# Two exps trade places on ScalarE in the second half of the last head

## The chip, the cores and the metric

The kernel runs on one core of a Trainium2 chip. The metric is the device time of one execution in microseconds, of which the profiled span is 1.7 to 2.8 us less. Executions of one kernel scatter by 3 to 4 us here, so the median of a few runs is given for time.

## The reference, cut to what matters

One token goes through layer norm, attention over a cache of 32768 keys and values in each of 32 heads of 192, an output projection with residual, and a small MLP with residual.

```
q = (layernorm(x) @ wq).reshape(32 heads, 192)
scores = einsum("hd,hkd->hk", q, k_cache) * 192**-0.5
p = softmax(scores)
o = einsum("hk,hkd->hd", p, v_cache)
h = x + o.reshape(1, 6144) @ wo
out = h + relu(layernorm(h) @ w1) @ w2
```

Keys and values are 825 MB, and each is used once. Reading them is the bulk of the time: the DMA row of the page is at 90% or more in every slice but the last, at 429 GB/s over the span.

Of the kernel before, what the change touches and what calls it, by code (L numbers as in the profile page):

```python
# [80 lines left out]
def kernel(  # L81
# [48 lines left out]
    def chunks(h):  # L130
        return ends if h == LAST else full
# [469 lines left out]
    def copies(g, h, c):  # L601
        ld, off, jc, jp = chunks(h)[c][:4]
        t0 = sum(len(tiles(q[3])) for q in chunks(h)[:c])
        for k, (b0, nb) in enumerate(tiles(jp)):
            g.wait("T", h, c, k)
            src = tp[(t0 + k) % TP]
            g.do(lambda: act.copy(out=kT[c % 2][:, b0:b0 + nb, :], in_=src[:, 0:nb, :].bitcast(bf16)),  # L607
                 "act_pe", ("cp", h, c, k))

    def exp_pe(g, h, c):  # L610
        jp = chunks(h)[c][3]
        g.wait("S", h, c)
        g.do(lambda: act.activation(out=pB[c % NB][:, 0:jp], in_=sp[:, 0:jp], func=F.Exp, scale=SCALE,  # L613
                                    accum_out=dsums[:, 2 * c + 1:2 * c + 2]), "act_pe", ("ep", h, c))

    def exp_dve(g, h, c):
        ld, off, jc, jp = chunks(h)[c][:4]
        jd = jc - jp
        if jd == 0:
            return  # L620
        g.wait("sc", h, c)
        g.do(lambda: act.activation(out=pA[c % NB][:, 0:jd], in_=sc[c % NC][:, 0:jd], func=F.Exp, scale=SCALE,  # L622
                                    accum_out=dsums[:, 2 * c:2 * c + 1]), "act_pe", ("ed", h, c))

    def q_wide(g, h):
        g.wait("qs", h)
        if h > 0:
            g.wait("sc", h - 1, NC - 1)
        g.do(lambda: act.copy(out=qb[:], in_=mm[:, 0:Dh]), "act_dve", ("qb", h))
        g.do(lambda: act.copy(out=qm[:], in_=mm[:, Dh:Dh + 12]), "act_pe", ("qm", h))  # L630
# [13 lines left out]
    def act_head(g, h):  # L644
        q_wide(g, h)

        n = len(chunks(h))
        for c in range(n):
            if c == 4 and h < LAST:
                exp_pe(g, h, 3)  # L650
                exp_dve(g, h, 3)
                copies(g, h, 4)
                continue
            copies(g, h, c)
            if h == LAST:
                if c > 5:
                    exp_dve(g, h, c - 2)
                if c > 2:
                    exp_pe(g, h, c - 1)
                if c < 2:  # L660
                    exp_pe(g, h, c)
                    exp_dve(g, h, c)
                elif 2 < c < 5:
                    exp_dve(g, h, c - 1)
            elif c > 0:
                exp_pe(g, h, c - 1)
                exp_dve(g, h, c - 1)
        if h == LAST:
            exp_dve(g, h, n - 2)
        exp_pe(g, h, n - 1)  # L670
        exp_dve(g, h, n - 1)

    def act_end(g):
        act_head(g, LAST)
        act_norm(g, "ln2")
        g.wait("h1")
        g.wait("rs", "ln2")
        g.do(lambda: act.activation(out=h1T[:], in_=o_ps[:, 0:FT], func=F.Relu, scale=ln_t["ln2"]["rs"][:]),
             "act_pe", ("h1T",))
# [118 lines left out]
    for f in (dma_program, pool_program):  # L798
        f(plan)
    parts = {"pe": (pe_start, pe_head, pe_end), "act": (act_start, act_head, act_end), "dve": (dve_start, dve_head, dve_end)}  # L800
    logs, links = {}, {}
    for e, (start, head, end) in parts.items():
# [13 lines left out]
    for e in parts:  # L816
        far = {s: 0 for s in TAKEN[e]}
        ends_at[e] = []
        for h in range(LAST):
            for label in logs[e][h]:  # L820
                s, n = at[label]
# [86 lines left out]
```

## The kernel before: what the change and the argument touch

Each head is worked in chunks of keys. In a chunk some rows' scores are made on VectorE (multiply by the query into `pr`, reduce into `sc`); the others on TensorE: transposes into PSUM (`tp`), copies of them to SBUF by ScalarE (`kT`), then matmuls with two columns into the PSUM bank `sp`. ScalarE takes the exp of both: `exp_pe` of TensorE's scores (`sp` to `pB`), `exp_dve` of VectorE's (`sc` to `pA`). TensorE then multiplies both with the values into `o_ps`.

The last head has ten chunks, numbered 0 to 9; "the second half" is chunks 6 to 9. Its ScalarE program:

```
def act_head(g, h):
    q_wide(g, h)
    n = len(chunks(h))
    for c in range(n):
        ...                                # cut: chunk 4 of the other heads
        copies(g, h, c)                    # kT <- tp, waits for transposes of chunk c
        if h == LAST:
            if c > 5:
                exp_dve(g, h, c - 2)       # waits for VectorE's scores of chunk c-2
            if c > 2:
                exp_pe(g, h, c - 1)        # waits for TensorE's scores of chunk c-1
            ...                            # cut: chunks 0 to 4
    if h == LAST:
        exp_dve(g, h, n - 2)
    exp_pe(g, h, n - 1)
    exp_dve(g, h, n - 1)
```

There is one `sp` bank, so TensorE's scores of a chunk wait for the exp of the chunk before:

```
def scores_pe(g, h, c):
    g.wait("cp", h, c, ...)                # its copies
    if c > 0:
        g.wait("ep", h, c - 1)             # exp_pe of the chunk before has read sp
    ...
```

TensorE's order at the end:

```
        scores_pe(g, h, 6)
        transposes(g, h, 8)
        scores_pe(g, h, 7)                 # waits for exp_pe(6)
        transposes(g, h, 9)
        values(g, h, 4)
        scores_pe(g, h, 8)
        scores_pe(g, h, 9)                 # waits for exp_pe(8) and copies(9)
        for c in (5, 6, 7):
            values(g, h, c)
        den_mm(g, h)                       # sums of all exps
        values(g, h, 8)
        values(g, h, 9)
        ...                                # cut: scaling, projection, norm, MLP
```

The softmax here doesn't subtract the row's maximum and nothing guards it: scores larger than these inputs give would overflow.

## Time and profile before

| | before |
|---|---|
| median of 3 runs | 1922.56 us (1920.89 to 1924.06) |
| profiled span | 1920.8 us |
| last load that the chain names ends | 1850.08 us |
| VectorE's last scores end | 1902.59 us |
| last value product ends | 1909.87 us |
| from there to the end | 10.9 us |

The page's first part gives each engine's busy time. No engine is near full, and this says nothing about the end of the program: the average covers the 1850 us up to the last load that the chain names, in which the DMA row is full.

```profile
PE 1558.5 (81%) x15890; PEld 1090.5 (57%) x15890; DVE 1563.3 (81%) x732; ACT 938.0 (49%) x1998; POOL 1.0 (0%) x6
```

The DMA row, the chain of waits in order of time, the timeline of the last 30 us and the clock windows are shown and read in the prediction. PE is TensorE's matmuls, PEld its weight loads, DVE VectorE, ACT ScalarE, POOL GpSimd; a q behind such a name is that engine's sequencer. In the timeline a line is: start, duration, engine, source line, operation, output and input, count, and in brackets how long the engine idled before it and what ended that.

### The profile page before, as it was taken

What the parts mean: (1) busy time and instruction counts of PE and PEld (TensorE: products, weight loads), DVE (VectorE), ACT (ScalarE), POOL (GpSimd) and SP (SyncE); (2) the same over time, 40 slices, a digit from 0 to 9 for tenths busy, and PEclk for the clock granted to TensorE, in tenths of its full rate; (3) what the DMA queues carried; (4) which work ended last, traced back from release to release, by engine and by line L of the source; (5) the groups of instructions that cost most, each with busy time, mean ns of one, the idle gap of its engine ahead of it and who ended that gap; (6) DMA issues with size and microseconds to landing.
All of it is one profiled execution on the core that took longest, in us unless ns stands there. A gap on an engine that the chain in (4) does not pass through costs nothing.

```text
span 1920.8 us, 36095 instructions
## 1 busy us (share of the span) xinstructions
PE 1558.5 (81%) x15890; PEld 1090.5 (57%) x15890; DVE 1563.3 (81%) x732; ACT 938.0 (49%) x1998; POOL 1.0 (0%) x6
## 2 busy tenths in 40 slices
PE   7778787887888788888878878878788788888787
PEld 7555555555555565655555556555555556555554
DVE  2797787987878978789887889878798787897896
ACT  2455454554544554545545545535455455455453
POOL 0000000000000000000000000000000000000000
PEclk9888998888988889888899887899888898888898
DMA  9999999999999999999999999999999999999997
GB/s 410 425 437 427 430 438 430 440 427 436 432 434 432 439 429 431 436 431 441 427 440 427 437 429 436 438 426 437 431 437 427 441 428 439 428 436 437 427 433 320
DMA packets 29634, 825.29 MB, mean 430 GB/s; under 512 B 3115, under 2 KB 4652, under 8 KB 8108
## 3 DMA queue, kind: packets, MB, share of 16 engines
q1 hardware_dynamic: 29610, 824.98, 99.6%
q8 instruction: 15, 0.25, 0.0%
q14 instruction: 7, 0.06, 0.0%
q10 hardware_dynamic: 2, 0.00, 0.0%
HBM read 824.97 MB, written 0.00 MB: 429 GB/s over the span
## 4 chain that ended last, share of the span: by engine, by line
DVE 42%; DMA 37%; PE 14%; ACT 5%; issue 1%; DVEq 0%; POOLq 0%; SPq 0%
DMA kt<-in_A_k_cache_dram 35%; DVE sc L704 20%; DVE pr L701 20%; PE o_ps L364 7%; PE tp L383 6%; ACT kT L607 4%; DMA va<-in_A_v_cache_dram 2%; DVE o_pair L716 1%; PE sp L364 1%; ACT pA L622 0%; DVE oT L726 0%; DMA kt<-in_A_wq_dram 0%; DVE rec L709 0%; DVE rec L710 0%; DVE odd L722 0%
## 5 line engine op out<-in xcount | busy, mean ns | idle before, releaser
L701 DVE TENSOR_TENSOR pr<-kt,qb 128x3072 f32<-128x3072 bf16 (+2 forms) x257 | 757.5, 2948 | 314.9 <-POOLq L325 286.8
L607 ACT COPY kT<-tp 128x1024 bf16<-128x1024 bf16 (+1 forms) x897 | 812.9, 1016 | 276.8 <-PE tp L383 276.8
L383 PE MATMUL tp<-ident_f,kt 128*128 128x128 f32 x3453 | 590.9, 332 | 237.6 <-POOLq L346 163.2
L704 DVE TENSOR_REDUCE sc<-pr 128x16 f32<-128x3072 f32 (+2 forms) x257 | 756.9, 2945 | 8.9
L383 PEld LDWEIGHTS tp<-ident_f,kt 128*128 128x128 f32 x3453 | 486.0, 171 | 288.1 <-POOLq L346 168.9
L364 PE MATMUL o_ps<-va,pB 128*2 128x384 bf16 x1150 | 223.8, 343 | 62.8 <-POOLq L346 62.8
L364 PEld LDWEIGHTS sp<-qm,kT 128*128 128x128 bf16 x6906 | 197.6, 98 | 84.6 <-issue 42.8
L364 PE MATMUL sp<-qm,kT 128*128 128x2 bf16 x6906 | 214.4, 164 | 27.5 <-ACT pB L613 26.1
L364 PE MATMUL o_ps<-vb,pB 128*2 128x384 bf16 x1152 | 214.5, 332 | 22.2 <-ACT pA L622 21.6
L622 ACT ACTIVATE pA<-sc 128x16 bf16<-128x16 f32 (+2 forms) x257 | 58.0, 226 | 349.7 <-DVEq L65 349.7
L613 ACT ACTIVATE pB<-sp 128x16 bf16<-128x16 f32 (+2 forms) x258 | 51.8, 201 | 306.0 <-PE sp L364 306.0
L364 PEld LDWEIGHTS o_ps<-va,pB 128*2 128x2 bf16 x1150 | 94.5, 87 | 159.6 <-POOLq L346 70.3
L364 PE MATMUL o_ps<-va,pA 128*2 128x384 bf16 x898 | 174.9, 337 | 0.0
L364 PE MATMUL o_ps<-vb,pA 128*2 128x384 bf16 x896 | 166.7, 326 | 0.0
L364 PEld LDWEIGHTS o_ps<-vb,pB 128*2 128x2 bf16 x1152 | 90.2, 85 | 122.6 <-ACT pA L622 27.7
L364 PEld LDWEIGHTS o_ps<-va,pA 128*2 128x2 bf16 x898 | 78.4, 87 | 78.7 <-issue 13.6
L364 PEld LDWEIGHTS o_ps<-vb,pA 128*2 128x2 bf16 x896 | 75.3, 84 | 70.3
L613 ACT ACTIVATION_READ_ACCUMULATOR pB<-sp 128x1 f32 x258 | 54.8, 212 | 0.0
L622 ACT ACTIVATION_READ_ACCUMULATOR pA<-sc 128x1 f32 x257 | 52.8, 205 | 0.0
L364 PE MATMUL o_ps<-xn_ln,kt 128*96 128x1 bf16 (+1 forms) x316 | 22.3, 208 | 2.7 <-DMA kt<-in_A_wq_dram 2.7
L364 PEld LDWEIGHTS o_ps<-xn_ln,kt 128*96 128x96 bf16 (+1 forms) x316 | 22.1, 174 | 2.8 <-issue 2.7
L716 DVE TENSOR_SCALAR o_pair<-o_ps,rec 2x384 bf16<-2x384 f32 x32 | 19.4, 605 | 2.7 <-PE o_ps L364 1.7
(69 smaller groups left out, 186.8 us busy)
## 6 DMA issues: line engine op xcount, KB each, us to landing
kt<-in_A_k_cache_dram SPq DMA_DIRECT2D x62, 6144.0 KB, 26.7
vb<-in_A_v_cache_dram SPq DMA_DIRECT2D x63, 3072.0 KB, 20.8
va<-in_A_v_cache_dram SPq DMA_DIRECT2D x31, 6144.0 KB, 26.8
kt<-in_A_k_cache_dram SPq DMA_DIRECT2D x3, 3072.0 KB, 21.0
wo_s<-in_A_wo_dram SPq DMA_DIRECT2D x16, 480.0 KB, 19.0
kt<-in_A_wq_dram SPq DMA_DIRECT2D x4, 1536.0 KB, 10.9
va<-in_A_v_cache_dram SPq DMA_DIRECT2D x1, 3072.0 KB, 23.1
va<-in_A_v_cache_dram SPq DMA_DIRECT2D x2, 1536.0 KB, 34.0
```

Of the source, the lines that this page charges most:

```text
L364: return lambda: pe.matmul(o, lhsT=w, rhs=r, **kw)
L383: calls.append(lambda b=b, o=o: pe.transpose(out=dst[:, b, :], in_=src[:, o:o + 2 * P].bitcast(f32), identity=ident_f[:]))
L607: g.do(lambda: act.copy(out=kT[c % 2][:, b0:b0 + nb, :], in_=src[:, 0:nb, :].bitcast(bf16)), "act_pe", ("cp", h, c, k))
L613: g.do(lambda: act.activation(out=pB[c % NB][:, 0:jp], in_=sp[:, 0:jp], func=F.Exp, scale=SCALE, accum_out=dsums[:, 2 * c + 1:2 * c + 2]), ...
L622: g.do(lambda: act.activation(out=pA[c % NB][:, 0:jd], in_=sc[c % NC][:, 0:jd], func=F.Exp, scale=SCALE, accum_out=dsums[:, 2 * c:2 * c + ...
L701: g.chain(lambda: dve.tensor_tensor(out=pr[:, 0:j1 - j0, :], in0=src[:, (off + j0) * Dh:(off + j1) * Dh].rearrange("p (j d) -> p j d", d=D ...
L704: g.chain(lambda: dve.reduce_sum(out=sc[c % NC][:, j0:j1], in_=pr[:, 0:j1 - j0, :], axis=X), "dve")
L716: g.do(lambda: dve.tensor_scalar_mul(out=o_pair[:, :, 1, :], in0=o_ps[0:2, 0:2 * Dh].rearrange("q (i d) -> q i d", i=2), scalar1=rec[0:2, ...
```

## The change

Its intent: VectorE's scores come late, TensorE's early; ScalarE's program has the late exp first, and in the trace the early one stood behind it with its input ready (2.06 us, from 1889.69 to 1891.75, and 0.99 us, from 1898.13 to 1899.12); so the early exp goes in front of the late one, and TensorE gets its `sp` bank back sooner.

```
             if h == LAST:
+                if c > 2:
+                    exp_pe(g, h, c - 1)
                 if c > 5:
                     exp_dve(g, h, c - 2)
-                if c > 2:
-                    exp_pe(g, h, c - 1)
...
+        exp_pe(g, h, n - 1)
         if h == LAST:
             exp_dve(g, h, n - 2)
-        exp_pe(g, h, n - 1)
         exp_dve(g, h, n - 1)
```

Five pairs trade places: one behind each of the copies of chunks 6, 7, 8 and 9, and one at the end. The order on the other engines is unchanged.

More of the change, by code (lines that the diff above doesn't have):

```diff
@@ L655, in act_head @@
             if h == LAST:
+                if c > 2:
+                    exp_pe(g, h, c - 1)
                 if c > 5:
                     exp_dve(g, h, c - 2)
-                if c > 2:
-                    exp_pe(g, h, c - 1)
                 if c < 2:
@@ L667, in act_head @@
                 exp_dve(g, h, c - 1)
+        exp_pe(g, h, n - 1)
         if h == LAST:
             exp_dve(g, h, n - 2)
-        exp_pe(g, h, n - 1)
         exp_dve(g, h, n - 1)
```

## The prediction

> **What bounds the kernel now.** I read the page first: the 40 slices, then the chain of waits.
>
> ```profile
> DMA  9999999999999999999999999999999999999997
> HBM read 824.97 MB, written 0.00 MB: 429 GB/s over the span
> DVE 42%; DMA 37%; PE 14%; ACT 5%; issue 1%; DVEq 0%; POOLq 0%; SPq 0%
> ```
>
> The DMA row is full in every slice but the last: the kernel streams 825 MB at a nearly constant 430 GB/s, and no order on ScalarE changes that. The change concerns only the last head, after the loop, so it can gain or lose only where loading no longer sets the end. So next I read the chain of waits in order of time, from 1850 us of the 1920.8 us span.
>
> ```profile
> 1833.98 16.10 DMA kt<-in_A_k_cache_dram
> ...
> 1850.23 3.37 DVE pr L701
> ...
> 1897.07 1.76 DVE sc L704
> ...
> 1898.92 0.30 ACT pA L622 x2
> 1899.22 0.16 ACT pB L613 x2
> 1899.38 0.05 issue
> 1899.43 0.45 PE sp L364 x12
> 1899.88 7.62 PE o_ps L364 x36
> ```
>
> The last load that the chain names ends at 1850.08. From there VectorE multiplies and reduces without a break (L701, L704) up to 1898.82; then the chain crosses ScalarE in 0.46 us and stays on TensorE: scores (sp), then the value products (o_ps) to 1909.87. The remaining 10.9 us are a serial tail (scaling, projection, norm, MLP, output). So the end is set by when TensorE finishes the value products, and the crossing on ScalarE is what the change edits. The timeline of the second half shows the crossing:
>
> ```profile
> 1891.53 0.22 ACT L622 ACTIVATE pA<-sc 128x16 bf16<-128x16 f32 x1 [0.58 <-DVEq L65]
> 1891.75 0.16 ACT L613 ACTIVATE pB<-sp 128x12 bf16<-128x12 f32 x1
> ...
> 1892.06 0.60 PE L364 MATMUL sp<-qm,kT 128*128 128x2 bf16 x18 [1.65 <-ACT pB L613]
> ...
> 1898.92 0.21 ACT L622 ACTIVATE pA<-sc 128x8 bf16<-128x8 f32 x1 [1.84 <-DVEq L65]
> ...
> 1899.12 0.16 ACT L613 ACTIVATE pB<-sp 128x8 bf16<-128x8 f32 x1
> ...
> 1899.43 0.45 PE L364 MATMUL sp<-qm,kT 128*128 128x2 bf16 x12 [1.29 <-ACT pB L613]
> ```
>
> Read the brackets as a chain. ScalarE idles for VectorE's scores (0.58 and 1.84 us), does that exp (pA), then the exp of TensorE's scores (pB), and TensorE, idle for 1.65 and 1.29 us, goes on only then: its next scores overwrite the one sp bank that pB reads. VectorE and TensorE each finished long before, but TensorE pays for VectorE's lateness, because ScalarE's instructions run in program order. The scores behind the pB of 1891.75 ended at 1889.69, those behind the pB of 1899.12 at 1898.13.
>
> [...] cutting the last 80 us into such windows gives
>
> ```profile
> 1890.09:1893.50 3.41, 1.76 (x29) 1.28 (x28) 3.23 (x3) 2.72 (x8) 0.00 (x0) 1.00 0.99 415
> 1893.50:1896.92 3.42, 3.42 (x13) 1.39 (x12) 3.27 (x2) 1.70 (x6) 0.00 (x0) 0.51 1.01 425
> 1896.92:1900.33 3.41, 2.12 (x33) 1.26 (x32) 3.15 (x3) 0.61 (x5) 0.00 (x0) 0.99 1.00 410
> 1900.33:1903.74 3.41, 3.41 (x13) 1.36 (x12) 2.23 (x2) 1.04 (x5) 0.00 (x0) 0.51 1.03 418
> ```
>
> Each line has the window's length, busy TensorE, weight loads, VectorE, ScalarE and GpSimd, then the granted clock: full, half, full, half. The windows with the two waits above are each followed by one at half clock, where a value matmul comes every 0.32 us in place of 0.163. Over some 80 windows of this trace the next one is at half clock when transposes and value matmuls (two-column score matmuls left out) filled less than about 1.45 us of it, and at full clock from about 1.5 us; those two windows had 1.36 us each. That threshold is my reading of this trace.
>
> **The change part by part.** Nothing is added or removed; on ScalarE four exps of TensorE's scores, with their accumulator reads, trade places in chunks 6 to 9 (plus the last one at the end), and no other engine's order changes. Chunk by chunk, with durations from the timeline:
> - Copies of chunk 6: the exp goes out some 0.2 us earlier, but TensorE does not wait for it there (scores follow transposes at 1889.10 directly). Worth 0. VectorE's exp is 0.2 us later; its user starts at 1892.6. Costs 0.
> - Copies of chunk 7 end at 1890.95. The exp of scores 6 (ready since 1889.69) now runs at once, to about 1891.2, so scores 7 start at 1891.25 in place of 1892.05: 0.8 us. Transposes 9 and values 4 follow directly (values 4 from 1892.65 in place of 1893.31).
> - Copies of chunk 8 still stand behind VectorE's exp of chunk 5 (its sc is ready at 1891.45), so they stay near 1891.8 to 1893.2; the exp of scores 7 then runs to 1893.45. Scores 8 need it only after values 4. No wait.
> - Copies of chunk 9 still stand behind VectorE's exp of chunk 6 (sc ready at 1895.13), so they run from 1895.4 to 1896.9. Scores 9 need them and the exp of scores 8, which runs at once behind them: about 1897.15 to 1897.2. So scores 9 may start there in place of 1899.43, and values 5 at about 1897.6 in place of 1899.81: **2.2 us at most**. This wait remains of the old one.
> - In between lies the pace of values 4: 16 matmuls. At half clock for 10 of them, as now, they took 4.37 us: 1892.65 + 4.37 = 1897.0, scores 8 and 9 run to about 1898.1, and the gain is 1.7 us. At full clock 16 × 0.163 = 2.6 us, end at 1895.3, and the wait for the copies counts instead: 2.2 us.
> - From values 5 on: 36 value matmuls before the denominator (16 + 10 + 10), now 7.62 us, of which some 10 ran at half clock (about 1.65 us extra). At full clock 36 × 0.163 = 5.9 us, so a further 1.7 us: 2.2 + 1.7 = 3.9 us.
>
> In the phase of the clock windows of this profile, window 1890.09 to 1893.50 would hold 1.16 us of transposes and 0.85 us of values, about 2.0 us, well over 1.5; so values 4 and 5 both run at full clock: **3.9 us**, value products done at about 1906.0. [...] Where both kernels happen to escape the half clock, 1.6 to 1.7 us is left; where values 5 still runs partly cold, about 2.3. I sum to a mean gain of **2.5 us**: 1922.56 − 2.5 = **1920.0 us**.
>
> **The rivals.**
> - *The loads take over.* Values need their last chunk: issued at 1871.8, landed 29.6 us later, 1901.4, used from about 1905. The first MLP weights land at 1888.2 + 17.9 = 1906.1 and are used from about 1908.7; the last (issued 1893.7, 17.2 us) at 1910.9, used from about 1912.2. All hidden, with 1.3 us to spare in the tightest, so no more than 5 us could be gained at all. If they bit, the gain would stop near 3: 1919.5.
> - *VectorE becomes the bound.* Its last scores end at 1902.59 and their exp at 1902.97, whatever ScalarE does; the denominator and the last 12 value matmuls need it. The new schedule reaches them at 1903.5 at the earliest, 0.6 us later. Close, so this caps the gain near 4.5 us; it does not take it away.
> - *Only the wait moves.* The copies behind VectorE's exps remain. If scores 9 waited as long for them as for the exp, the gain would be 0: 1922.5. Against it: copies of chunk 9 end 1.8 us before VectorE's next exp.
> - *Lost in noise.* Three runs before span 3.2 us, as large as the gain; a median may hide it.
>
> **Range and chances.** Gain 1.6 to 4.0 us by phase, plus about 1 us of scatter in each median: 1917.3 to 1922.5. Two per cent are 38 us; the whole part touched lasts under 35 us, and it cannot shrink below VectorE's own chain. Faster 0.005, within 2% 0.99, slower 0.005.
>
> **What would show it right or wrong.** Right: scores 7 start within 0.3 us of the end of the exp after copies 7; TensorE's wait of 1.65 us falls to about 0.8; the wait of scores 9 names the copies or an exp straight behind them, not one behind VectorE's; values 4 and 5 lie mostly at a granted clock of 1.0; value products end 1.6 to 4 us earlier before the tail, and the tail stays 10.9 us. VectorE's idle time before its denominator falls from 5.27 us to between 1.3 and 3.6. Wrong: a wait of value matmuls on a load, MLP matmuls waiting on DMA, or a half-clock window on values 5 as long as before.

The pB of 1891.75 had its input ready for 2.06 us, since 1889.69. "Such windows" are stretches of 3.41 us that begin within 0.1 us of where this trace's clock changes lie or would lie on the same grid. 2.2 us of waiting and 1.7 us of pace make 3.9 us in this profile's phase; with my estimates for other phases, 1.6 to 1.7 and 2.3 us, I came to 2.5 us in the mean and 1920.0 us. That other executions have other phases was an assumption then; the later traces show it (2.60, 2.71 and 1.88 us in three of the kernel before).

## The result, and the profile after

| | before | after |
|---|---|---|
| median, runs of the same rounds | 1922.95 us (4 runs, 1920.89 to 1924.06) | 1918.91 us (4 runs, 1918.39 to 1920.26) |
| profiled span | 1920.8 us | 1916.9 us |
| last value product ends | 1909.87 us | 1905.80 us |

The ratio is 0.9981, 95% interval 0.9964 to 0.9999: the same within 2%, and 3.6 us shorter in the mean. Ratios here are the mean time of one kernel's runs over that of the other's of the same rounds, so not quite the ratio of the medians.

First the page of the kernel after. Loading is as before, and so are the shares of the chain: nothing that fills the first 1850 us has moved.

```profile
DMA  9999999999999999999999999999999999999998
HBM read 824.97 MB, written 0.00 MB: 430 GB/s over the span
DVE 42%; DMA 37%; PE 14%; ACT 5%; issue 1%; DVEq 0%; POOLq 0%; SPq 0%
```

The chain of waits of the kernel after, in order of time (start, duration, what):

```profile
1833.88 16.09 DMA kt<-in_A_k_cache_dram
...
1850.12 3.37 DVE pr L701
...
1893.27 1.76 DVE sc L704
...
1895.11 0.30 ACT pA L622 x2
1895.41 1.39 ACT kT L607 x2
1896.80 0.18 ACT pB L613 x2
1896.98 0.05 issue
1897.03 0.45 PE sp L364 x12
1897.48 5.94 PE o_ps L364 x36
```

The chain now leaves VectorE one chunk earlier: after the reduce that ends at 1895.03, not the one that ended at 1898.82. It crosses ScalarE through three operations and not two: VectorE's exp of chunk 6, the copies of chunk 9 behind it, the exp of TensorE's scores. TensorE's 36 value matmuls take 5.94 us where they took 7.62. So scores 9 start 2.3 us earlier, once the 0.11 us are taken off by which the whole last head starts sooner in this trace (1850.12 against 1850.23), and a further 1.68 us went out of a block of work whose instructions are the same.

The timeline of the kernel after, at the two waits of TensorE:

```profile
1891.07 0.21 ACT L613 ACTIVATE pB<-sp 128x12 bf16<-128x12 f32 x1
...
1891.42 0.60 PE L364 MATMUL sp<-qm,kT 128*128 128x2 bf16 x18 [0.78 <-ACT pB L613]
...
1895.11 0.21 ACT L622 ACTIVATE pA<-sc 128x8 bf16<-128x8 f32 x1 [1.82 <-DVEq L65]
...
1896.69 0.19 ACT L613 ACTIVATE pB<-sp 128x8 bf16<-128x8 f32 x1
...
1897.03 0.45 PE L364 MATMUL sp<-qm,kT 128*128 128x2 bf16 x12 [1.21 <-ACT pB L613]
```

The first wait fell from 1.65 to 0.78 us. The second is nearly as long (1.21 us, before 1.29), but begins and ends more than two microseconds earlier: the engine named is the exp, yet the time is spent in the copies of chunk 9, which start when VectorE's exp of 1895.11 is done.

Cut into the clock windows of this run, which begin 0.4 us earlier than in the first trace (columns as in the prediction: window, its length, busy TensorE, weight loads, VectorE, ScalarE, GpSimd, granted clock, DMA share, GB/s):

```profile
1889.75:1893.16 3.41, 2.63 (x41) 1.99 (x39) 3.26 (x2) 3.35 (x11) 0.00 (x0) 1.00 1.00 421
1893.16:1896.58 3.42, 2.65 (x26) 1.37 (x24) 3.24 (x3) 1.60 (x6) 0.00 (x0) 1.00 1.00 417
1896.58:1899.99 3.41, 2.96 (x28) 1.71 (x29) 3.15 (x3) 0.85 (x7) 0.00 (x0) 1.00 1.01 418
```

Before, 1893.50 to 1896.92 and 1900.33 to 1903.74 were at half clock (0.51). Here the three windows hold 2.1 to 2.6 us of transposes and value matmuls each (the busy TensorE above counts the two-column scores too), and the clock stays at 1.00 from 1882.93 to 1910.23.

### The profile page after: what moved, and what is told of

It reads as the page before. It is cut to its first block, busy times and chain, and to the rows that moved or that the text cites. A ratio compares the mean times of both kernels' runs of the same rounds, so it can differ in the third digit from the quotient of the medians.

```text
span 1916.9 us, 36096 instructions
## 1 busy us (share of the span) xinstructions
PE 1549.2 (81%) x15890; PEld 1083.9 (57%) x15890; DVE 1563.2 (82%) x732; ACT 938.9 (49%) x1998; POOL 1.0 (0%) x6
## 4 chain that ended last, share of the span: by engine, by line
DVE 42%; DMA 37%; PE 14%; ACT 5%; issue 1%; DVEq 0%; POOLq 0%; SPq 0%
DMA kt<-in_A_k_cache_dram 35%; DVE sc L704 20%; DVE pr L701 20%; PE o_ps L364 7%; PE tp L383 6%; ACT kT L607 5%; DMA va<-in_A_v_cache_dram 2%; DVE o_pair L716 1%; PE sp L364 1%; ACT pA L622 0%; DVE oT L726 0%; DMA kt<-in_A_wq_dram 0%; DVE rec L709 0%; DVE rec L710 0%; DVE odd L722 0%
## 6 DMA issues: line engine op xcount, KB each, us to landing
kt<-in_A_wq_dram SPq DMA_DIRECT2D x4, 1536.0 KB, 10.9
```

## The experiments

**Theory.** The gain is two things that feed each other: TensorE's waits for its `sp` bank end earlier (chunks 7 and 9 alone matter), and, because value work then fills the two windows that held 1.36 us of transposes and values each, as the prediction cuts them, and were followed by half clock (0.51), the 3.4 us at half clock twice over vanish. **Rivals.** Order alone, without the clock; all five swaps carrying a part; VectorE or the loads capping the gain.

**A measure that is free of the loads' scatter.** In the twelve traces of the experiments and the two first ones, VectorE's first multiply of the last head starts between 1849.97 and 1851.62 us, when the keys have come. That moves the whole end and has nothing to do with the order on ScalarE. So I compare the *stretch*, from that start to the start of the scaling of `o_ps`, 0.03 us behind the last value product. Before: 1909.91 − 1850.23 = 59.68 us. After: 1905.83 − 1850.12 = 55.71 us. VectorE's last scores end 52.35 to 52.37 us into the stretch in every trace but that of the last experiment, where their amount is changed, so the stretch measures what follows from the order alone. The phase of a trace is the time of its clock changes modulo 3.413 us: in each of the two first traces all changes lie, to within 4 ns, on a grid of that step.

| run | stretch | phase | time: median, ratio with interval |
|---|---|---|---|
| before, first trace | 59.68 | 2.60 | 1922.95 |
| after, first trace | 55.71 | 2.18 | 1918.91, 0.9981 (0.9964 to 0.9999) |
| e1, swap behind copies 9 only | 56.92 | 2.34 | 1920.36, 0.9992 (0.9978 to 1.0005) |
| e2, swap behind copies 7 only | 59.61 | 3.03 | 1923.78, 1.0007 (0.9993 to 1.0021) |
| e3, swaps 7 and 9 | 56.18 | 0.67 | 1919.30, 0.9986 (0.9973 to 1.0000) |
| e9, swaps 6, 8 and end | 59.67 | 2.10 | 1922.52, 0.9999 (0.9986 to 1.0013) |
| e4, filler work, order of before | 57.99 | 0.47 | 1922.41, 1.0005 (0.9991 to 1.0018) |
| e10, filler again | 59.38 | 2.80 | 1922.36, 1.0000 (0.9987 to 1.0014) |
| e11, filler, one look | 58.00 | 0.31 | one run |
| e5, before again, one look | 59.68 | 2.71 | one run |
| e12, before again, one look | 59.68 | 1.88 | one run |
| e6, after again, one look | 55.71 | 1.71 | one run |
| e7, after, and copies first | 55.28 | 0.06 | 1919.44, 0.9986 (0.9972 to 1.0000) |
| e8, e7 and four rows moved | 54.34 | 2.20 | 1918.42, 0.9982 (0.9968 to 0.9996) |

All outputs are right. The runs e1 to e4 shared a chip and the runs of the kernel before, and so did e5 to e8, and e9 to e12.

### Which swaps matter: e1, e2, e3, e9

The edit is one condition, here for chunk 9 alone; for the others the set is (7,), (7, 9), and (6, 8) together with the swap at the end.

```
-                if c > 5:
+                if c > 5 and c not in (9,):
                     exp_dve(g, h, c - 2)
                 if c > 2:
                     exp_pe(g, h, c - 1)
+                if c > 5 and c in (9,):
+                    exp_dve(g, h, c - 2)
```

> Only the swap behind the copies of chunk 9 is made. Theory (waits in order, then clock): values 4 stay at half clock and end at 1897.7 as before, scores 8 end at 1898.1, scores 9 start at about 1898.5 instead of 1899.43, so the window of 1896.9 to 1900.3 holds about 2.2 us of value work and values 5 run at full clock: 0.9 us from the wait plus 1.7 us from the clock, 2.6 us faster than before in a run with before's window phase. Rival (order alone, no clock): 0.9 us. Rival (all swaps matter alike): about 1.0 us, a quarter of 3.9.

Measured: the stretch fell by 2.76 us. In its timeline values 4 are cold (at half clock) and values 5 are not:

```profile
1895.00 2.63 PE L364 MATMUL o_ps<-va,pB 128*2 128x384 bf16 x10
...
1898.53 0.45 PE L364 MATMUL sp<-qm,kT 128*128 128x2 bf16 x12
1899.35 0.45 PE L364 MATMUL sp<-qm,kT 128*128 128x2 bf16 x12 [0.36 <-ACT pB L613]
1899.73 1.46 PE L364 MATMUL o_ps<-va,pB 128*2 128x384 bf16 x8
```

Ten value matmuls of values 4 took 2.63 us where 1.79 us is the pace at full clock; scores 9 wait 0.36 us for the exp of scores 8, which goes out as soon as those end; then the first eight matmuls of values 5 take 1.46 us, where the kernel before needed 2.17. Scores 9 start 1.08 us earlier in the stretch, and 1.68 us come behind them: the theory's 0.9 + 1.7 us. In this trace order alone (0.9) and equal quarters (1.0) are both excluded; the timed runs, whose interval includes no change, cannot tell them apart.

> Only the swap behind the copies of chunk 7 is made. Theory: scores 7 start 0.8 us earlier and values 4 run at full clock and end near 1895.3, but the exp of scores 8 still stands behind VectorE's exp of chunk 7 (1898.9), so scores 9 start at 1899.4 as before, values 5 are cold as before, and the end does not move: 0.0 us (within 0.3). Rival (the saved 0.8 us and 1.7 us of clock in values 4 pass through to the end): 0.8 to 2.5 us faster.

Measured: the stretch is 59.61, 0.07 us less. TensorE's first wait is short (0.78 us), values 4 run at full clock, and everything gained is waited away:

```profile
1892.23 0.60 PE L364 MATMUL sp<-qm,kT 128*128 128x2 bf16 x18 [0.78 <-ACT pB L613]
...
1896.92 0.45 PE L364 MATMUL sp<-qm,kT 128*128 128x2 bf16 x12 [0.67 <-ACT pB L613]
1900.61 0.46 PE L364 MATMUL sp<-qm,kT 128*128 128x2 bf16 x12 [3.24 <-ACT pB L613]
1901.00 2.72 PE L364 MATMUL o_ps<-va,pB 128*2 128x384 bf16 x8
```

The wait of scores 9 grew from 1.29 to 3.24 us, because its end is set elsewhere: 1900.61 lies 49.21 us into the stretch, against 1899.43 − 1850.23 = 49.20 us before. An end that VectorE sets cannot be reached sooner by arriving sooner. Values 5 are cold, as before. The timed runs were slower than before in the mean by 1.4 us, with an interval that includes no change; its one trace has the last head starting 1.2 us late and nothing else. Why it would start late was not found.

> Both swaps, chunks 7 and 9, and no other. Theory: the whole gain, value products done within 0.2 us of the changed kernel's, but for the exp of scores 7, which stands behind VectorE's exp of chunk 6 (1895.2) and delays scores 8 by some 0.4 us; these have 1 us to spare before the copies of chunk 9 end. So 3.6 to 3.9 us faster in the profile's phase. Rival (the swaps at chunks 6, 8 and the end carry a part): clearly less, 2.6 us or so.

Measured: 56.18, 3.50 us less, just under what was expected. Here a half-clock window (1884.83 to 1888.24, phase 0.67) fell on transposes 6 and values 3, which no other trace of the new order had there: the first eight matmuls of values 3 took 2.71 us and not 1.46. So scores 7 came late and scores 9 followed. The rest, e9, makes sure that nothing is missing:

> Only the swaps that the two others leave: behind the copies of chunks 6 and 8, and the last two exps. Theory: none of these exps is waited for (scores 6 and 8 start straight after work that TensorE has anyway, the last exp is 4 us early), so the stretch from VectorE's first multiply of the last head to the end of the value products stays between 57.9 and 59.7 us according to the phase of the clock windows, as before, and the span is that of before. Rival (each swap carries a quarter of the gain): 1 to 2 us less.

Measured: 59.67. The three swaps at chunks 6 and 8 and at the end are worth nothing. Chunks 7 and 9 are the change.

### Is the clock a cause of its own? e4, e10, e11

The order on ScalarE is that of before, and TensorE gets work to do in its two waits, whose result nobody reads:

```
+    def fill(g, n):
+        for _ in range(n):
+            g.do(mmul(mm[0:2, P:P + 2 * Dh], ident_b[:, 0:2], va[:, 0:2 * Dh], start=True, stop=True))
...
         transposes(g, h, 8)
+        fill(g, 8)
         scores_pe(g, h, 7)
...
         scores_pe(g, h, 8)
+        fill(g, 6)
         scores_pe(g, h, 9)
```

> The order of before on ScalarE, but TensorE does 8 value-like matmuls into an unused part of a PSUM bank in its wait before scores 7, and 6 in its wait before scores 9; results are unchanged. Theory: scores 9 still start at 1899.4, but both windows hold over 1.5 us of work, so values 4 and 5 run at full clock, and the end comes 1.7 us earlier though no wait was shortened. Rival (clock does not matter, or is not set by this work): 0, or later by up to 0.5 us for the added work.

Measured: 57.99, 1.69 us less.

```profile
1899.16 0.45 PE L364 MATMUL sp<-qm,kT 128*128 128x2 bf16 x12 [1.91 <-ACT pB L619]
1899.55 1.46 PE L364 MATMUL o_ps<-va,pB 128*2 128x384 bf16 x8
```

Scores 9 start 1899.16 − 1849.97 = 49.19 us into the stretch, within a hundredth of before (49.20). No wait ended earlier, TensorE did more work, and the value products ended 1.69 us sooner. That the clock is a cause of its own, of that size, is shown in this trace. But five timed runs did not show it.

> The filler matmuls again, because its five timed runs (1920.7 to 1923.6) did not show the 1.7 us that its trace did. Theory: the stretch is 58.0 us in every phase, since both windows hold work; the scatter of the time is in when VectorE's first multiply of the last head can start (1850.0 to 1851.4 in the traces so far), which the loads set. Then the mean of ten runs of it is about 0.5 to 1.7 us under that of the kernel before. Rival (some windows still go to half clock in most phases, or the filler slows something else): stretch over 58.5 in this trace, and a mean equal to before.

> A third trace of the filler kernel: theory 58.0 us of stretch whatever the phase; rival more than 58.5.

Measured: 59.38 and 58.00. So "58.0 whatever the phase" was wrong. The windows of e10 around the second wait:

```profile
1897.20:1900.61 3.41, 1.70 (x20) 0.79 (x18) 3.15 (x3) 1.56 (x6) 0.00 (x0) 1.00 1.00 416
1900.61:1904.03 3.42, 3.22 (x21) 1.49 (x22) 3.33 (x2) 0.14 (x2) 0.00 (x0) 0.50 1.03 417
```

Of the 1.70 us, 1.14 are filler and 0.25 are values 4; the rest is two-column score matmuls. 1.39 us is under the 1.45 us that I had read from the trace of before, and the next window is at half clock: six filler matmuls were too few for this phase. That the times of the filler kernel (mean 1922.4 over both runs) are no lower than those of before (1922.0 and 1921.9) I cannot explain fully: two of three traces gain 1.7 us and one gains 0.3, and the timed runs leave no trace to read. What the filler is worth on average stays open; the next part has a hint.

### Does the phase wander? e5, e6, e12

> The kernel before once more, for a second trace of it. Theory: [...] their phase against the kernel differs from the first trace (where they began at 2.60 us modulo 3.413); the value products then end 59.7 us after VectorE's first multiply of the last head where values 4 and 5 are both hit by half clock, and down to 57.9 us where neither is. Rival (the phase is tied to the kernel): the same phase as before and 59.7 us again.

> The changed kernel once more, for a second trace. Theory: another phase, and a stretch from VectorE's first multiply of the last head to the end of the value products of 55.7 us (first trace) up to 57.3 us where the half clock hits part of the values. Rival (phase tied to the kernel): 55.7 again with the phase of the first trace.

> A third trace of the kernel before, for another phase of the clock windows. Theory: 59.7 us where both values 4 and 5 are hit by a half-clock window (phases near 2.6 us modulo 3.413, as in the two traces so far), 57.9 to 58.1 us where the window cut falls so that only one or none is, about the middle of the cycle. Rival: 59.7 in every phase.

Measured: the phases wander, 0.06 to 3.03 us in the fourteen traces, so they are not tied to the kernel. Yet all traces with the order of before at these places (three of before, and e9) stand at 59.67 or 59.68, with phases from 1.88 to 2.71, and both of the kernel after at 55.71. I have not seen a trace of the kernel before that escapes a half-clock window. That the phases of these four lie within one quarter of the cycle may be chance. The timed runs hint that some executions do escape: of the 27 of the kernel before that ran beside the experiments, 9 have spans of 1918.6 to 1919.4 us, but the earliest start seen in any trace (1849.97), a stretch of 59.68 and its tail of 10.9 us make 1920.5. Either the last head starts over 1 us earlier in these than in any trace, or their stretch is shorter; if the latter, it is no wonder that the filler's times are not lower. The timed runs leave no trace to tell.

### What limits the kernel after: e7, e8

e7 puts the copies of chunks 8 and 9 in front of VectorE's waiting exps too, and takes these exps later:

```
             copies(g, h, c)
             if h == LAST:
+                if c == 9:
+                    exp_dve(g, h, 5)
                 if c > 2:
                     exp_pe(g, h, c - 1)
-                if c > 5:
-                    exp_dve(g, h, c - 2)
+                if c == 6:
+                    exp_dve(g, h, 4)
...
+        exp_dve(g, h, n - 4)        # last head only, as n - 3 and n - 2 below
         exp_pe(g, h, n - 1)
+        exp_dve(g, h, n - 3)
         exp_dve(g, h, n - 2)
         exp_dve(g, h, n - 1)
```

> The changed kernel, and besides the copies of chunks 8 and 9 go in front of VectorE's waiting exps of chunks 5 and 6. Theory (what remains of the wait is that copies of chunk 9 stand behind VectorE's exp of chunk 6): scores 9 start straight after the exp of scores 8, about 0.9 us earlier than in the changed kernel, and then the denominator waits for VectorE's last exp (2.45 us after its last reduce starts 1.75 us of work), so only 0.4 us of it reaches the end: stretch 55.3 us. Rival (TensorE alone is the bound): 54.8 us. Rival (the copies were not what scores 9 waited for): 55.7 us, no change.

Measured: 55.28, 0.43 us less. Scores 9 wait 0.36 us for the exp of scores 8 and for nothing else, and the wait shows up where it was expected, at the denominator:

```profile
1903.48 0.40 PE L364 MATMUL mm<-dsums,ones_mat 128*128 128x20 f32 x2 [0.91 <-ACT pA L622]
```

The exp that it waits for (pA) is that of VectorE's last scores. VectorE is now the limit, so e8 takes four rows of chunk 5 from it:

```
-    ends = [(c // 2, (c % 2) * J, J, JPS[c % 2] if c > 3 else 16) for c in range(NC - 2)]
+    ends = [(c // 2, (c % 2) * J, J, JPS[0] if c > 3 else 16) for c in range(NC - 2)]
```

> As the run with copies first, and besides four key rows of chunk 5 go from VectorE to TensorE (20 and 12 instead of 16 and 16), where TensorE and ScalarE idle over 1 us anyway. Theory: VectorE's last scores come 1.76 us earlier, the denominator does not wait any more, stretch 54.8 us, 0.9 us under the changed kernel; the last MLP weights, which land near 1911, are then needed within 0.2 us of their landing, so the loads come within reach of setting the end. Rival (loads set the end already): the stretch falls but the tail behind it grows by as much and the span stays. Rival (TensorE's added transposes cost more than VectorE's time saves): stretch of 55.3 us or more.

Measured: 54.34, 1.37 us under the kernel after, more than the 0.9 expected. VectorE's last scores end 50.76 us into the stretch, 1.6 us sooner, and the denominator does not wait. The tail behind the stretch is 11.27 us, against 11.07 after, and in it the second MLP product halts:

```profile
1909.97 1.40 PE L364 MATMUL attT<-h1T,kt 128*128 128x1 bf16 x44 [0.36 <-ACT h1T L683]
1911.60 0.58 PE L364 MATMUL attT<-h1T,kt 128*128 128x1 bf16 x16 [0.23 <-issue]
```

The profile puts the gap of 0.23 us down to "issue", and its cause stays open. The last weights, asked for at 1894.0, landed 17.6 us later, at 1911.6, when the matmuls went on. But in the kernel the first matmul that waits for these weights is the 51st of the 60; it started at 1911.78, six behind the gap. And in e6 the same product pauses before its 54th matmul, 1.2 us after its last load had landed. The loads are near all the same: the 31st matmul, the first to need the load before the last, started at 1910.83, just as that one landed (1893.13 + 17.7 us). Whether a shorter stretch would buy anything further is not shown. e8 is the fastest of all by its trace (span 1916.5) and by its median, but 1918.42 against 1918.91 are of different calls with other runs of before beside them; between it and the kernel after the times decide nothing. Against the kernel before it is clear of noise.

## Why the prediction was right

**What bounds the kernel.** Right: loading until 1850, VectorE's chain, the crossing on ScalarE, TensorE's values, a serial tail. The tail is 11.07 us, 0.2 more than before. Up to the issue of the output store it took as long as before (7.46 and 7.48 us), so the 0.2 lie behind that issue; in e6, with the same tail, they lie in the second MLP product (1.97 us in place of 1.76). No cause of either was found.

**The waits.** "Scores 7 start at 1891.25": 1891.42 in the trace, with its wait at 0.78 us, as said ("falls to about 0.8"). By the stretch they start 0.5 us earlier than before, and 1.1 us in e6, where 0.8 was said. "Copies of chunk 9 run from 1895.4 to 1896.9": 1895.32 to 1896.80. "Scores 9 at about 1897.15": 1897.03, in a run whose last head starts 0.11 us sooner. The wait of scores 9 names an exp straight behind the copies. Chunks 6, 8 and the end were put at 0, and e9 found 0.

**The clock.** "Values 4 and 5 both run at full clock: 3.9 us, value products done at about 1906.0": 1905.80, and 3.97 us less of the stretch. The step from "waits shorten" to "the window is then fuller than 1.5 us" to "the next one is not cold" held in the kernel after at these two places. In every trace of the new order (after, e3, e6, e7, e8) the first ten matmuls of values 4 took 1.79 us and the first eight of values 5 were at the same pace (1.46 us, or ten in 1.79); with the order of before at both places (before, e5, e9, e12) the ten took 3.09 to 3.33 us and the eight 2.14 to 2.63. The filler shows it apart from the order in two of its three traces (1.7 us less). The threshold was read too widely, though. In the 80 windows that it was read from it holds, to within 0.1 us, for those that ran at full clock themselves. At half clock more was not always enough: this window of the kernel before, here with its transposes alone (busy TensorE, weight loads, ScalarE, then clock, DMA share and GB/s), held 2.62 us of them and was followed by half clock.

```profile
828.55:831.96 3.41, 2.62 (x12) 2.15 (x12) 3.41 (x5) 0.50 1.12 483
831.96:835.38 3.42, 2.78 (x14) 2.49 (x13) 3.21 (x4) 0.50 1.06 460
```

Even windows at full clock went either way. In the two first traces, from 60 to 1907 us and each cut on the grid of its own clock changes, all that held less than 1.36 us of transposes and value matmuls were followed by half clock, and all with more than 1.51 us by full clock. Between the two both happened: 1.51 us of transposes was followed by half clock (after, 1531.36 to 1534.77), 1.36 us of values by full clock (before, 1286.01 to 1289.42). The busy time of TensorE as a whole did not tell them apart: a window with 2.76 us busy, but 1.17 us of values and the rest two-column scores, was followed by half clock (before, 992.46 to 995.88), one with 1.42 us busy, all transposes, by full clock (after, 548.32 to 551.73). No rule that fits all of them was found. In the first trace of the kernel after the windows around values 4 and 5 ran at full clock and held 2.1 us or more, so the step does not hang on the exact number.

**The mean.** The prediction summed over phases to "a mean gain of 2.5 us", with part of the phases giving only 1.6 to 1.7, "where both kernels happen to escape the half clock". Both traces of the kernel after gave 3.97, and no trace of before escaped the half clock, so against the traces the 2.5 is too low. The timed runs cannot say so: they gave 3.6 us in the mean with an interval of 0.2 to 6.9, and against the 27 later runs of the kernel before (mean 1922.05) the gain is 2.9. As the spans of these hint that some executions do escape, the weights of the phases stay open. The result, 1918.91, is inside the range and 1.1 us under the predicted time; that it is so close is partly luck, given the scatter.

**The rivals.** The loads did not set the end in the kernel after, but of the 1.3 us "to spare in the tightest" only 0.3 were left in its first trace: the last weights landed at 1911.6 (issued at 1894.2, 17.4 us), and the first matmul to need them started at 1911.9. VectorE "caps the gain near 4.5 us": e7 ran into that cap, at 59.68 − 55.28 = 4.40 us. VectorE's idle time before its denominator fell from 5.27 to 1.31 us, the low end of what was given.

## What to carry to other kernels

Where an engine's program puts something late before something ready, as ScalarE's did here for 2.06 us, put what is ready first, and judge each such swap by whose arrival ends the wait: of five swaps here one made room, one was worth something only together with it, and three were worth nothing. Where a wait shortens on TensorE, look at the granted clock of the matmuls behind it: here windows with waits of 1.65 and 1.29 us were each followed by one at 0.51, and 1.7 us of the 4.0 in these traces came from there. Where runs scatter by as much as the effect, measure from an event in the trace that the change cannot move.
